# Three token columns per W2 chunk in group 0, a later first block of the tail, and three moved steps

## The chip, the cores and the metric

The kernel runs on one core of a Trainium2 chip. The metric is the device time of one execution in microseconds (us), smaller is better. One execution of the kernel before was also recorded by the hardware profiler; times "at 75.26" are us from the start of that record's span.

## What is computed

Inputs are q, k, v of shape (8, 8, 576, 64) in float32 (batch, heads, tokens, head size), a gain vector of 512, W1 (512 x 2048) and W2 (2048 x 512). The output is (8, 576, 512) in float32.

```python
# causal attention in a sliding window of 64 tokens
scores = scale * np.matmul(q, k.transpose(0, 1, 3, 2))
rel = pos[:, None] - pos[None, :]
mask = (rel >= 0) & (rel < 64)
attn = softmax(np.where(mask, scores, -1e9))
x = np.matmul(attn, v).transpose(0, 2, 1, 3).reshape(B, S, H * D)
# a layer norm and a two-layer MLP with a residual
mu = np.mean(x, axis=-1, keepdims=True)
var = np.mean((x - mu) ** 2, axis=-1, keepdims=True)
xn = (x - mu) / np.sqrt(var + 1e-06) * g_ln
out = x + np.maximum(xn @ w_ch1, 0.0) @ w_ch2
```

## The kernel before

**Groups and blocks.** The first 512 tokens of each of the 8 batches make groups 0 to 7; the last 64 tokens of all batches together make group 8, the tail. A group has four blocks of 128 tokens. Attention is done block by block, then the MLP for the group's 512 tokens at once. Matrix operands are float16, sums are float32.

**Attention of a block (g, j).** `s_mm` (L260) makes the scores on TensorE into two PSUM banks "sc" (for group 0 after a first product that writes the mask's bias), and ScalarE turns each bank into `pt` by Exp (L293). `s_mask` multiplies `pt` by the mask on VectorE. `b_step` (L302) multiplies `pt` by the values (16 products, L320) into the bank `xps`, of which there is one, and VectorE divides and takes mean and variance (L323 to L331). The values are there twice: `vA` has blocks of 128 tokens, `vB` the same rows shifted by 64 partitions. `z_step` normalizes the block, `zt_step` (L355) transposes it into `zT`, on TensorE with a copy out of PSUM for groups 0 and 1, by a transposing DMA on SP's queue from group 2 on. For groups 0 and 1 `vB` is filled by small copies on VectorE or ScalarE (`vB_cur`, `vB_prev`), which read the loaded float32 values `v32` directly; from group 2 on `make_vB` fills it from `vA` by two DMAs on GpSimd's queue. There is one buffer for `v32`, so `load_v` of a group waits until the group before has copied from it. GpSimd casts q, k, v, W1 and W2 from float32 to float16.

**MLP.** In groups 0 and 1 layer 1 runs in half tiles (`l1_half`, bank `hph`, tokens 0 to 255 and 256 to 511) and then whole ones (`l1`, bank `hps`); ScalarE applies Relu into `hrT`. Layer 2 of group 0 is four sums over 16 hidden chunks, one for each block of 128 tokens (a "token column", `ch`). W2 arrives in eight loads of two hidden chunks each, cast by `w2_cast` in that order. `l2_two` (L544) does columns 0 and 1 in step with the chunks, column 1 one chunk behind; `l2` does columns 2 and 3 after them. `add_out` adds the residual on VectorE and `store` issues the output DMA on SP. From group 1 on layer 2 is a Strassen-like form of seven products (`stage`, L492), in the order 1, 2, 6, 5, 7, 4, 3, two halves each; sums of operands are made on VectorE (`s_sums`, `w2_sums`), and several products add into one bank, with `post` (L482) on VectorE reading it in between. In the tail layer 1 has seven products too (`l1_product`, L560), on sums `zS` (`z_sums`, L695) and `w1S`.

**PSUM.** Eight banks: two "sc" (`ps_s`), two for `xps`, two for transposes ("t0" and "t1", `ps_t`), two "mm" (`ps_mm`) for products. `t_tile` (L74) alternates t0 and t1; while `tbank["shared"]` is set it uses t0 alone, since a product sits in t1.

**Order.** Every engine works through its instructions in the order in which the program writes them. The order is written by hand: the MLP of group g is a list of `units`, and `at(i, f, ...)` (L837) puts a step of the attention of the next group, a load or a cast behind unit i. Group 0 has 16 units of layer 1 (0 to 15), 9 of `l2_two` (16 to 24) and 8 of `l2` (25 to 32). Group 7 has 16 units of layer 1 and 14 of `stage`. `begin_last` (L822) starts the tail inside group 7; the rest of the tail runs from the generator `plan`. `keep_clock` puts extra products on TensorE during the start.

Of the kernel before, what the change touches and what calls it, by code (L numbers as in the profile page):

```python
# [10 lines left out]
FP32 = mybir.dt.float32  # L11
# [9 lines left out]
def kernel(  # L21
# [10 lines left out]
    nc = tc.nc  # L32
    B, H, S, D = q.shape
    DM = H * D
# [222 lines left out]
                    nc.tensor.transpose(out=tp[:, r, hp, :], in_=src[:, r, 2 * hp:2 * hp + 2, :], identity=ident16)  # L257
        evac(0, tailT[i][x], tp)

    def s_mm(g, j, pe_mask=False):  # L260
        sc = [ps_s.tile([128, NHP, 2, 64], FP32, tag="sc", name=f"sc_{g}_{j}_{par}") for par in range(2)]
        pt = p_pt.tile([128, 2, NHP, 2, 64], FP16, tag="pt", name=f"pt_{g}_{j}")
        pts[(g, j)] = pt
        if pe_mask:
            m = mbias[:, :]
            mb = bass.AP(tensor=m.tensor, offset=m.offset, ap=[m.ap[0], [0, NHP * 2], m.ap[1]])
            for par in range(2):
                nc.tensor.matmul(
                    out=sc[par][:, :].rearrange("p h w i -> p (h w) i"), lhsT=ident16, rhs=mb,
                    start=True, stop=False, skip_group_check=True,  # L270
                )
        for hp in range(NHP):
            for iw in range(2):
                for par in range(2):
                    rows = slice(64 * par, 64 * par + 64)
                    if g == NGRP - 1:
                        lhsT = tailT[j][1][rows, iw, hp, :]
                        rhs = tailT[j][0][rows, hp, 64 * iw:64 * iw + 64]
                    else:
                        w = 2 * j + iw  # L280
                        lhsT = qkT[g][1][rows, hp, 64 * w:64 * w + 128]
                        rhs = qkT[g][0][rows, hp, 64 * w:64 * w + 64]
                        if g >= XQ:
                            qb = flat(g)[rows, SM * hp + 16 * w:SM * hp + 16 * w + 16]
                            rhs = bass.AP(tensor=qb.tensor, offset=qb.offset, ap=[qb.ap[0], [128, 4], [1, 16]])
                    nc.tensor.matmul(out=sc[par][:, hp, iw, :], lhsT=lhsT, rhs=rhs,  # L286
                                     start=not pe_mask, stop=True, skip_group_check=pe_mask)
        for par in range(2):
            o, i = pt[:, par], sc[par][:, :]
            if XQ <= g < NGRP - 1:  # L290
                o = o.rearrange("p h w (r j) -> p (h w) r j", j=4)
                i = i.rearrange("p h w (j r) -> p (h w) r j", j=4)
            nc.scalar.activation(out=o, in_=i, func=AF.Exp, bias=0.0, scale=scale)  # L293

    def s_mask(g, j):
        pt = pts[(g, j)]
# [91 lines left out]
            eng.tensor_scalar(out=ab, in0=ab, scalar1=-1.0, scalar2=1.5, op0=ALU.mult, op1=ALU.add)  # L388
            eng.tensor_tensor(out=rs, in0=rs, in1=ab, op=ALU.mult)

    def mlp_units(g, split=0, two=False, seven=True):
        hrT = p_hrt.tile([128, NHC, 512], FP16, tag="hrT", name=f"hrT_{g}")
        hv = hrT[:, :, :].rearrange("p (c e) t -> p c e t", e=2)
        sS = {}
# [24 lines left out]
        def add_out(kb):  # L419
            xv = x_norm[(g, kb // 2)][:, kb % 2, :]  # L420
            if g < 2:
                nc.vector.scalar_tensor_tensor(
                    out=xv, in0=ch[kb], scalar=rstd[g][:, kb:kb + 1], in1=xv, op0=ALU.mult, op1=ALU.add,
                )
            else:
                nc.vector.tensor_tensor(out=xv, in0=ch[kb], in1=xv, op=ALU.add)
            store(kb)
# [113 lines left out]
            nc.scalar.activation(out=hrT[:, 2 * i:2 * i + 2, 256 * half:256 * half + 256], in_=hps,  # L541
                                 func=AF.Relu, bias=0.0, scale=1.0)

        def l2_two(i):  # L544
            for kb in range(2):
                e = i - kb
                if e == 0:
                    ch[kb] = ps_mm.tile([128, DM], FP32, tag="mm", name=f"ch_{g}_{kb}")
                if 0 <= e < NHC // 2:
                    for hc in (2 * e, 2 * e + 1):  # L550
                        nc.tensor.matmul(
                            out=ch[kb], lhsT=hrT[:, hc, 128 * kb:128 * (kb + 1)], rhs=w2s[:, hc, :],
                            start=(hc == 0), stop=(hc == NHC - 1),
                        )
                if e == NHC // 2 - 1:
                    add_out(kb)

        lbank = {}

# [31 lines left out]
        def l1_quad(d, e, h):  # L591
            return hv[:, 2 * d:2 * d + 2, e, 256 * h:256 * h + 256]
# [10 lines left out]
            eng.tensor_scalar(out=o, in0=o, scalar1=0.0, scalar2=None, op0=ALU.max)  # L603

        def l1_a(d):
            l1_product(1, d)
            l1_keep("s1", "A", d)
            l1_product(2, d)
            l1_sum(l1_quad(d, 0, 0), "B", "s1", d)
            l1_product(5, d)  # L610
            l1_keep("s5", "C", d)

# [13 lines left out]

        if last:
            def plan():
                yield
                l1_b(0)  # L630
                for d in range(1, 4):
                    l1_a(d)
                    l1_c(d - 1)
                    l1_b(d)
                    l1_e(d - 1)
                    if d == 2:
                        s_sums(0, 4, 1)
                stage(1, 0)
                s_sums(0, 4, 2)
                l1_c(3)  # L640
                s_sums(4, 8, 1)
                stage(1, 1)
                l1_e(3)
                s_sums(4, 8, 2)
                stage(2, 0)
                stage(2, 1)
                stage(6, 0)
                s_sums(0, 4, 3)
                stage(6, 1)
                s_sums(4, 8, 3)  # L650
                stage(5, 0)
                s_sums(0, 4, 4)
                stage(5, 1)
                s_sums(4, 8, 4)
                for n in (7, 4, 3):
                    for p in range(2):
                        stage(n, p)
                yield
            l1_a(0)
            return plan(), s_sums  # L660

        for half in range(2):
# [2 lines left out]

        for hc in range(split, NHC):
            units.append(lambda hc=hc: l1(hc))
        if two:
            for i in range(NHC // 2 + 1):
                units.append(lambda i=i: l2_two(i))  # L670
        if not seven:
            for kb in range(2 if two else 0, 4):
                for part in range(4):
                    units.append(lambda kb=kb, part=part: l2(kb, part))
        else:
            for n in (1, 2, 6, 5, 7, 4, 3):
                for p in range(2):
                    units.append(lambda n=n, p=p: stage(n, p))
# [86 lines left out]
    cast_qk(0, 1)  # L765
    cast_v(0, 2, 3)
    cast_v(0, 3, 4)
    for i in range(8):
        w1_cast(i)

# [21 lines left out]
    vB_prev(0, 2, 0)  # L792
    s_mm(0, 2, True)
    zt_step(0, 0)
    vB_cur(0, 3, 0)
    zt_step(0, 1)
    b_step(0, 2)
    s_mm(0, 3, True)
    z_step(0, 2)


# [20 lines left out]
    def begin_last():  # L822
        nonlocal rest
        rest, _ = mlp_units(NGRP - 1)
        next(rest)

    rest = None
    TAILS = {3: [0], 5: [1], 7: [2, 3]}
    for g in range(NGRP):
# [11 lines left out]
        if g == 0:  # L841
            at(0, b_step, 0, 3)
            at(1, zt_step, 0, 2)
            at(3, zt_step, 0, 3)
            at(4, newton, 0, 0, 4)
            at(11, t_main, 1, 0, 0, 1)
            at(12, t_main, 1, 1, 0, 1)
            at(13, vB_cur, 1, 0, 1)
            at(13, vB_prev, 1, 0, 1)
            at(13, vB_cur, 1, 1, 1)  # L850
            at(13, vB_prev, 1, 1, 1)
            at(16, s_mm, 1, 0)
            at(16, s_mask, 1, 0)
            at(17, s_mm, 1, 1)
            at(17, s_mask, 1, 1)
            at(18, b_step, 1, 0)
            at(21, b_step, 1, 1)
            at(22, zt_step, 1, 0)
            at(25, zt_step, 1, 1)
            at(26, t_main, 1, 0, 1, 0)  # L860
            at(27, t_main, 1, 1, 1, 1)
            at(28, vB_cur, 1, 2, 0)
            at(28, vB_prev, 1, 2, 1)
            at(29, vB_cur, 1, 3, 0)
            at(29, s_mm, 1, 2)
            at(29, s_mask, 1, 2)
            at(30, s_mm, 1, 3)
            at(30, s_mask, 1, 3)
            at(30, load_v, 2, 0, 4)
            at(33, b_step, 1, 2)  # L870
        if g == 1:
            at(0, cast_qk, 2, 0)
            at(0, cast_qk, 2, 1)
# [59 lines left out]
                at((2, 7, 12, 17)[j], z_step, b, j)  # L933
                at((12, 12, 18, {3: 24, 5: 23}.get(b, 22))[j], zt_step, b, j)
        for n, i in enumerate(TAILS.get(g, ())):
            ts = (13, 13, 16, 21) if n else (1, 2, 5, 11)
            at(ts[0], s_mm, NGRP - 1, i)
            at(ts[1], s_mask, NGRP - 1, i)
            at(ts[2], b_step, NGRP - 1, i)
            at(ts[2], z_step, NGRP - 1, i)  # L940
            at(ts[3], zt_step, NGRP - 1, i)
# [34 lines left out]
        if g == NGRP - 2:  # L976
            at(0, w1_sums, 1, 2)
            at(3, w1_sums, 3)
            at(21, w1_sums, 4)
            at(26, z_sums, NGRP - 1, 1, 2)  # L980
            at(27, z_sums, NGRP - 1, 3, 4)
            at(27, begin_last)
        for i, u in enumerate(units):
            if g > 1 and i == 20:
                tbank["shared"] = True
            u()
            for f, a in slots[i]:
                f(*a)
# [30 lines left out]
```

## Time and profile before

| | |
|---|---|
| median of 4 runs | 310.26 us (309.7 to 310.4) |
| the profiled execution: its time | 310.56 us |
| the profiled execution: span | 308.4 us |
| instructions in the span | 7582 |
| granted TensorE clock | 0.999 |
| VectorE, ScalarE, GpSimd busy | 218.1, 151.8, 170.9 us |
| moved by DMA | 58.35 MB, mean 189 GB/s |

The span runs from the first to the last recorded instruction; 2.16 us of the profiled execution lie around it. Rows of the profile have the form: line, engine, operation, output<-inputs by the program's names, shape, count; then busy time and the mean of one, and the idle time of the engine ahead of them with what ended it. PE is TensorE's products, PEld its weight loads, DVE is VectorE, ACT is ScalarE, POOL is GpSimd, SP is SyncE; SPq and POOLq are those engines' DMA issues. A wait is put down to what ended last. Line numbers are those of the kernel before.

### The profile page before, as it was taken

How to read it: one execution, taken by the hardware profiler on the slowest of the kernel's cores; microseconds unless marked ns; L12 is line 12 of the kernel's file. 1: busy time of each engine (PE TensorE's matmuls, PEld its weight loads, DVE VectorE, ACT ScalarE, POOL GpSimd, SP SyncE). 2: the span in 40 equal slices, each digit the busy share in tenths (PEclk: the TensorE clock that was granted, in tenths of full speed). 3: DMA queues.
4: the chain of work that ended last, by engine and by line, in shares of the span. 5: the costliest groups of instructions: out<-in, count | busy, mean ns of one | idle time of the engine just before them, and what ended most of it. 6: DMA issues, size and time to landing. Idle time of an engine off the chain costs nothing.

```text
span 308.4 us, 7582 instructions
## 1 busy us (share of the span) xinstructions
PE 296.2 (96%) x3061; PEld 196.8 (64%) x3061; DVE 218.1 (71%) x411; ACT 151.8 (49%) x255; POOL 170.9 (55%) x255
## 2 busy tenths in 40 slices
PE   7988989999999999999999999999999999999992
PEld 4557545697454478646954786469646854688882
DVE  0677575865775996589666965896669675868972
ACT  2496635587326742866157527752475056215500
POOL 7578676555861798279805983698145507104300
PEclk9999999999999999999999999999999999999999
DMA  8999899999866997899289997983790396003014
GB/s 191 266 384 306 309 361 271 276 273 252 166 170 201 237 204 137 274 289 120 51 263 285 216 143 237 297 153 72 219 168 20 60 204 180 19 17 138 0 37 102
DMA packets 113669, 58.35 MB, mean 189 GB/s; under 512 B 83617, under 2 KB 104609, under 8 KB 113634
## 3 DMA queue, kind: packets, MB, share of 16 engines
q1 hardware_dynamic: 112576, 54.67, 72.4%
q0 software_dynamic: 768, 2.80, 3.8%
q8 instruction: 24, 0.39, 0.6%
q10 hardware_dynamic: 290, 0.40, 0.4%
q14 instruction: 11, 0.09, 0.1%
HBM read 38.80 MB, written 9.44 MB: 156 GB/s over the span
## 4 chain that ended last, share of the span: by engine, by line
PE 75%; DMA 15%; SPq 5%; DVE 1%; POOL 1%; issue 1%; POOLq 0%
PE hps L400 28%; PE pA L477 12%; PE pB L477 8%; PE pC L477 8%; PE ch L412 6%; DMA w2s<-in_moe_w_ch_dram 5%; DMA qk<-in_q_dram 4%; SPq L141 4%; PE xps L320 3%; PE sc L286 3%; DMA vB<-vA 3%; PE lA L586 2%; PE tp L229 2%; DMA w1s<-in_moe_w_ch_dram 2%; DMA v<-in_v_dram 1%; SPq L89 1%
## 5 line engine op out<-in xcount | busy, mean ns | idle before, releaser
L400 PE MATMUL hps<-zT,w1g 128*128 128x512 f16 x416 | 95.3, 379 | 0.0
L404 ACT ACTIVATE hrT<-hps 128x512 f16<-128x512 f32 x104 | 62.3, 599 | 39.3 <-PE hps L400 35.7
L400 PEld LDWEIGHTS <-w1g 128*128 128x128 f16 x416 | 38.6, 98 | 43.3 <-issue 0.7
L293 ACT ACTIVATE pt<-sc 128x512 f16<-128x512 f32 x72 | 39.0, 594 | 27.8 <-DVE xn L484 14.7
L477 PEld LDWEIGHTS <-sS 128*128 128x128 f16 x448 | 43.3, 98 | 5.8 <-issue 0.9
L350 POOL TENSOR_SCALAR rsz<-mvg 128x1 f32<-128x1 f32 x28 | 10.2, 363 | 60.2 <-DVE mvg L331 59.5
L128 POOL CAST qk<-qk 128x1024 f16<-128x1024 f32 x32 | 35.0, 1107 | 12.6 <-DMA qk<-in_q_dram 4.3
L477 PEld LDWEIGHTS <-hrT 128*128 128x128 f16 x336 | 32.4, 98 | 5.5 <-ACT hrT L625 0.3
L300 DVE TENSOR_TENSOR pt<-pt,mask 128x1024 f16<-128x1024 f16 x32 | 26.9, 847 | 9.0 <-ACT pt L293 9.0
L215 ACT COPY qkT<-tp 128x1024 f16<-128x1024 f16 x16 | 16.1, 1012 | 34.1 <-PE tp L229 34.0
L484 DVE TENSOR_TENSOR xn<-pA,xn 128x512 f32<-128x512 f32 x28 | 19.2, 684 | 17.4 <-PE pA L477 12.1
L477 PE MATMUL pA<-wT,sS 128*128 128x256 f16 x224 | 26.9, 272 | 0.7 <-DVE xn L484 0.7
L477 PE MATMUL pC<-w2s,sS 128*128 128x256 f16 x224 | 26.9, 273 | 0.0
L353 POOL TENSOR_SCALAR z<-xn,rsz 128x512 f16<-128x512 f32 x28 | 25.0, 893 | 2.9
L323 DVE RECIPROCAL rcp<-xps 128x8 f32<-128x8 f32 x36 | 7.4, 204 | 26.3 <-PE xps L320 26.3
L328 DVE BATCH_NORM_STATS2 stats<-xn 128x6 f32<-128x512 f32 x36 | 25.0, 694 | 1.2
L326 DVE TENSOR_TENSOR xn<-xps,rcp 128x512 f32<-128x512 f32 x36 | 24.9, 691 | 1.2
L451 DVE TENSOR_TENSOR sS<-hrT 128x512 f16<-128x512 f16 (+1 forms) x40 | 24.5, 612 | 0.6 <-ACT hrT L404 0.6
L536 PE MATMUL hph<-zT,w1g 128*128 128x256 f16 x192 | 23.3, 273 | 0.8 <-ACT zT L368 0.8
L412 PE MATMUL ch<-w2s,hrT 128*128 128x512 f16 x96 | 23.1, 380 | 0.0
L147 POOL CAST vA<-v 128x1024 f16<-128x1024 f32 (+2 forms) x19 | 17.3, 929 | 6.8 <-DMA v<-in_v_dram 6.8
L320 PEld LDWEIGHTS <-pt 128*64 128x64 f16 x576 | 12.2, 110 | 13.3 <-issue 5.9
(111 smaller groups left out, 444.7 us busy)
## 6 DMA issues: line engine op xcount, KB each, us to landing
out_dram<-xn SPq DMA_DIRECT2D x33, 256.0 KB, 2.4
qk<-in_q_dram SPq DMA_DIRECT2D x16, 512.0 KB, 6.3
qk<-in_k_dram SPq DMA_DIRECT2D x16, 512.0 KB, 7.1
v<-in_v_dram SPq DMA_DIRECT2D x32, 256.0 KB, 7.2
w2s<-in_moe_w_ch_dram SPq DMA_DIRECT2D x9, 512.0 KB, 9.3
w1s<-in_moe_w_ch_dram SPq DMA_DIRECT2D x4, 512.0 KB, 6.7
tk<-in_k_dram SPq DMA_DIRECT2D x8, 256.0 KB, 4.7
tv<-in_v_dram SPq DMA_DIRECT2D x8, 256.0 KB, 5.0
```

The costliest lines, as they stand in the source:

```text
L128: nc.gpsimd.tensor_copy(out=dst[:, :].rearrange("p (a j) e d -> p a e j d", j=j), in_=t[:, :].rearrange("p (a e j d) -> p a e j d", e=2, j ...
L293: nc.scalar.activation(out=o, in_=i, func=AF.Exp, bias=0.0, scale=scale)
L300: nc.vector.tensor_tensor(out=ptv, in0=ptv, in1=mb, op=ALU.mult)
L326: nc.vector.tensor_tensor(out=xn, in0=xps[:, :, 0:D], in1=rcp_b, op=ALU.mult)
L328: nc.vector.bn_stats(out=stats, in_=xv)
L353: nc.gpsimd.tensor_scalar(out=z, in0=xv, scalar1=rs, scalar2=nm, op0=ALU.mult, op1=ALU.add)
L400: nc.tensor.matmul(out=hps, lhsT=w1g[:, kc, 128 * hc:128 * (hc + 1)], rhs=zT[g][:, kc, :], start=(kc == 0), stop=(kc == NKC - 1),)
L404: nc.scalar.activation(out=hrT[:, hc, :], in_=hps, func=AF.Relu, bias=0.0, scale=1.0)
L412: nc.tensor.matmul(out=ch[kb], lhsT=hrT[:, hc, 128 * kb:128 * (kb + 1)], rhs=w2s[:, hc, :], start=(hc == 0), stop=(hc == NHC - 1),)
L451: nc.vector.tensor_tensor(out=o, in0=x, in1=y, op=op)
L477: nc.tensor.matmul(out=o, lhsT=a[:, c, 128 * p:128 * p + 128], rhs=wv[:, c, :], start=(first and (p == 0 or split_c) and c == 0), stop=(c ...
L536: nc.tensor.matmul(out=hps[:, e], lhsT=w1g[:, kc, 128 * hc:128 * (hc + 1)], rhs=zT[g][:, kc, 256 * half:256 * half + 256], start=(kc == 0) ...
```

## The change

- Group 0, layer 2: `l2_three` takes columns 0, 1 and 2 in step with the W2 chunks, each one chunk behind the one before. Column 2 accumulates in t1, so the transposes of group 1 use t0 alone from unit 17 until column 2 has ended (unit 25). Column 3 follows in four units. The list has 30 units instead of 33, and the steps of group 1 behind it are put 1 to 3 slots earlier.
- Start: the scores of block 3 of group 0 go into the two "mm" banks (`later`), ahead of `b_step(0, 2)` and `zt_step(0, 1)`; their two Exps are issued after `zt_step(0, 1)`. The vB copy of block 3 (64 rows) leaves ScalarE; the diff writes it on GpSimd, ahead of the casts of W1. The copy of block 3's `zT` out of PSUM goes from ScalarE to VectorE.
- Group 7: `b_step`, `z_step` and `zt_step` of the tail's block 3 are one slot later.
- Tail: `z_sums` are one slot later; of `l1_a(0)` the products 1 and 2 stay at slot 27, product 5 goes to slot 28, behind the first half of product 3 of group 7.

```diff
+    def s_mm(g, j, pe_mask=False, later=False):
+        sc = [(ps_mm if later else ps_s).tile([128, NHP, 2, 64], FP32, tag="mm" if later else "sc",
+                                              name=f"sc_{g}_{j}_{par}") for par in range(2)]
...
+        if later:
+            return exps
+        exps()
...
-        def l2_two(i):
-            for kb in range(2):
+        def l2_three(i):
+            for kb in range(3):
                 e = i - kb
-                if e == 0:
+                if e == 0 and kb == 2:
+                    ch[kb] = ps_t.tile([128, DM], FP32, tag="t1", name=f"ch_{g}_{kb}")
+                elif e == 0:
                     ch[kb] = ps_mm.tile([128, DM], FP32, tag="mm", name=f"ch_{g}_{kb}")
...
                 if e == NHC // 2 - 1:
                     add_out(kb)
+                    if kb == 2:
+                        tbank["shared"] = False
...
         def l1_a(d):
+            l1_a1(d)
+            l1_a2(d)
+
+        def l1_a1(d):
             l1_product(1, d)
             l1_keep("s1", "A", d)
             l1_product(2, d)
             l1_sum(l1_quad(d, 0, 0), "B", "s1", d)
+
+        def l1_a2(d):
             l1_product(5, d)
             l1_keep("s5", "C", d)
...
             def plan():
+                l1_a2(0)
                 yield
...
-            l1_a(0)
+            l1_a1(0)
             return plan(), s_sums
...
     cast_v(0, 3, 4)
+    nc.gpsimd.tensor_copy(out=vB[0][64:128, 3, :, 0:D], in_=v32[0][0:64, 3])
...
     s_mm(0, 2, True)
     zt_step(0, 0)
-    vB_cur(0, 3, 0)
+    exps3 = s_mm(0, 3, True, True)
+    b_step(0, 2)
     zt_step(0, 1)
-    b_step(0, 2)
-    s_mm(0, 3, True)
+    exps3()
     z_step(0, 2)
...
-        next(rest)
...
-            at(3, zt_step, 0, 3)
+            at(3, zt_step, 0, 3, "dve")
...
-            at(21, b_step, 1, 1)
-            at(22, zt_step, 1, 0)
-            at(25, zt_step, 1, 1)
-            at(26, t_main, 1, 0, 1, 0)
-            at(27, t_main, 1, 1, 1, 1)
-            at(28, vB_cur, 1, 2, 0)
-            at(28, vB_prev, 1, 2, 1)
-            at(29, vB_cur, 1, 3, 0)
-            at(29, s_mm, 1, 2)
-            at(29, s_mask, 1, 2)
-            at(30, s_mm, 1, 3)
-            at(30, s_mask, 1, 3)
-            at(30, load_v, 2, 0, 4)
-            at(33, b_step, 1, 2)
+            at(20, b_step, 1, 1)
+            at(21, zt_step, 1, 0)
+            at(23, zt_step, 1, 1)
+            at(24, t_main, 1, 0, 1, 0)
+            at(25, t_main, 1, 1, 1, 1)
+            at(25, vB_cur, 1, 2, 0)
+            at(25, vB_prev, 1, 2, 1)
+            at(26, vB_cur, 1, 3, 0)
+            at(27, s_mm, 1, 2)
+            at(27, s_mask, 1, 2)
+            at(28, s_mm, 1, 3)
+            at(28, s_mask, 1, 3)
+            at(27, load_v, 2, 0, 4)
+            at(30, b_step, 1, 2)
...
-            ts = (13, 13, 16, 21) if n else (1, 2, 5, 11)
+            ts = (13, 13, 17, 22) if n else (1, 2, 5, 11)
...
-            at(26, z_sums, NGRP - 1, 1, 2)
-            at(27, z_sums, NGRP - 1, 3, 4)
+            at(27, z_sums, NGRP - 1, 1, 2)
+            at(28, z_sums, NGRP - 1, 3, 4)
             at(27, begin_last)
+            at(28, lambda: next(rest))
...
-            if g > 1 and i == 20:
+            if i == (20 if g > 1 else 17 if g == 0 else -1):
                 tbank["shared"] = True
```

More of the change, by code (lines that the diff above doesn't have):

```diff
@@ L258, in t_tail @@
         evac(0, tailT[i][x], tp)
-    def s_mm(g, j, pe_mask=False):
-        sc = [ps_s.tile([128, NHP, 2, 64], FP32, tag="sc", name=f"sc_{g}_{j}_{par}") for par in range(2)]
+    def s_mm(g, j, pe_mask=False, later=False):
+        sc = [(ps_mm if later else ps_s).tile([128, NHP, 2, 64], FP32, tag="mm" if later else "sc",
+                                              name=f"sc_{g}_{j}_{par}") for par in range(2)]
         pt = p_pt.tile([128, 2, NHP, 2, 64], FP16, tag="pt", name=f"pt_{g}_{j}")
@@ L287, in s_mm, with exps @@
                                      start=not pe_mask, stop=True, skip_group_check=pe_mask)
[L288 to L293, printed above, removed]
+        def exps():
+            for par in range(2):
+                o, i = pt[:, par], sc[par][:, :]
+                if XQ <= g < NGRP - 1:
+                    o = o.rearrange("p h w (r j) -> p (h w) r j", j=4)
+                    i = i.rearrange("p h w (j r) -> p (h w) r j", j=4)
+                nc.scalar.activation(out=o, in_=i, func=AF.Exp, bias=0.0, scale=scale)
+        if later:
+            return exps
+        exps()
     def s_mask(g, j):
@@ L389, in newton, with mlp_units @@
             eng.tensor_tensor(out=rs, in0=rs, in1=ab, op=ALU.mult)
-    def mlp_units(g, split=0, two=False, seven=True):
+    def mlp_units(g, split=0, three=False, seven=True):
         hrT = p_hrt.tile([128, NHC, 512], FP16, tag="hrT", name=f"hrT_{g}")
@@ L667, in mlp_units @@
             units.append(lambda hc=hc: l1(hc))
-        if two:
-            for i in range(NHC // 2 + 1):
-                units.append(lambda i=i: l2_two(i))
+        if three:
+            for i in range(NHC // 2 + 2):
+                units.append(lambda i=i: l2_three(i))
         if not seven:
-            for kb in range(2 if two else 0, 4):
+            for kb in range(3 if three else 0, 4):
                 for part in range(4):
```

## The prediction

> **What bounds the kernel now.** I read the page's engine line first, then TensorE's own waits, then the chain of waits around the longest DMA in it, then the timelines of the stages that the edits touch. All times are us from the span's start, of one profiled execution.
>
> ```profile
> PE 296.2 (96%) x3061; PEld 196.8 (64%) x3061; DVE 218.1 (71%) x411; ACT 151.8 (49%) x255; POOL 170.9 (55%) x255
> PE warm L749 <- DVE mbias L742: 2.3, 1, 2.3
> PE ztp L365 <- DVE z L342: 1.1, 1, 1.1
> PE hph L536 <- ACT zT L368: 0.8, 1, 0.8
> PE pA L477 <- DVE xn L484: 0.7, 1, 0.7
> PE ch L551 <- POOL w2s L204: 0.7, 2, 0.5
> PE xps L320 <- DMA vB<-vA: 0.4, 1, 0.4
> ```
>
> TensorE is busy for 96% and this list is nearly all that it waits for before its last product. The edits do not change how many products it runs, so they can win at most four of these lines: 1.1 (at 18.0), 0.8 (at 25.5), 0.7 (at 43 to 45) and, in group 7, 0.7 (at 268). Together 3.3. The line that decides is the last one: a wait of 0.41 that no edit names.
>
> ```profile
> 45.68 1.05 POOL w2s L204
> ...
> 54.02 1.25 DVE vB L217
> ...
> 55.85 0.92 SPq L141
> ...
> 56.82 3.82 SPq L141
> ...
> 60.69 4.03 DMA v<-in_v_dram
> ...
> 64.86 1.91 POOL vA L147
> ...
> 67.06 8.06 DMA vB<-vA
> 75.12 0.14 issue
> 75.26 0.45 PE xps L320 x16
> ```
>
> This is the chain of waits (start, length). Block 0 of group 2 (`b_step(2, 0)`, slot 14 of group 1) cannot start before vB of group 2 has landed at 75.12; TensorE's product before it ends at 74.85. So whatever is won before 75 is kept only as far as that landing moves. The chain says that v's load begins after VectorE's vB copy at 54 to 55.3. But it stays in its queue: the last of four issues is held until 60.69. The window table says why (columns: stretch, PE, PEld, DVE, ACT and POOL busy, clock, DMA share, GB/s):
>
> ```profile
> 52.00:54.00 2.00, 2.00 (x26) 0.87 (x23) 1.88 (x2) 0.98 (x2) 1.10 (x2) 1.00 1.03 337
> 54.00:56.00 2.00, 1.93 (x32) 0.90 (x25) 1.93 (x2) 1.36 (x3) 0.98 (x1) 1.00 0.93 280
> 56.00:58.00 2.00, 2.00 (x26) 0.97 (x24) 1.16 (x2) 0.81 (x2) 1.48 (x2) 1.00 1.08 405
> 58.00:60.00 2.00, 2.00 (x32) 1.64 (x30) 1.90 (x5) 0.79 (x2) 1.46 (x4) 1.00 1.19 301
> 60.00:62.00 2.00, 2.00 (x30) 1.79 (x23) 1.90 (x5) 1.24 (x3) 0.00 (x0) 1.00 0.43 99
> ```
>
> The DMA engines are full (share 0.93 to 1.19) up to 60. The loads of q and k for group 2 were issued by 50.8 and are landing until 57.4 (GpSimd's casts wait for them), then three stores, then v; v's packets of 256 bytes start only at 58.0 although v was issued at 55.4. An earlier issue waits in the same line.
>
> **The change part by part.**
>
> *Start.* `s_mm(0,3)` (2 + 16 products, 0.88) moves ahead of `b_step(0,2)` and `zt_step(0,1)`, into ps_mm. It fills the 1.08 wait before `ztp` at 19.02. But its two exps now stand behind the copy of zT block 1 on ScalarE, and the first `hph` takes over one of its banks. ScalarE: exps of block 2 to 18.77, zT 0 to 19.3, (the 0.62 vB copy gone), zT 1 to 20.1, first exp of block 3 to 20.6. So `hph` starts at 20.65, before at 20.60: nothing won there; the other exp ends at 21.15, hidden by the first `hph` (0.87).
>
> *vB copy of block 3.* The title says VectorE; the diff writes `nc.gpsimd.tensor_copy`. No row has GpSimd copying across partitions; priced as its cast 128x512, 0.62 (bounds 0.5 and 1.2), between 15.80 and w1's cast at 16.65 (idle 0.85 there). VectorE runs `z` (0.49) in the same place. In the trace such pairs stretch the VectorE side: z takes 0.87 at 24.22 with GpSimd busy, 0.49 at 15.77 without. The Trainium skill's "SBUF — State Buffer" (Who interferes with whom) speaks against the edit more strongly: an exclusive lock, the later one blocks fully. By the row w1's casts keep their time; by the rule the copy ends at 16.9 and the first four casts are 0.3 late. Either is covered by the 1.21 that GpSimd waits for w1's DMA at 20.72; without that cover it costs 0.3.
>
> *zT of block 3 on VectorE.* Before, the ScalarE copy stood behind a Relu (25.74, 0.58). `b_step(0,3)` is some 0.3 earlier, z ends near 24.75, transposes by 25.0. The copy from PSUM on VectorE: 128x1024 f16 takes 1.22, so 0.61 (bounds 0.4 to 0.9). Second half of layer 1 starts at about 25.75 instead of 26.37: 0.62 won. Newton stands behind it and is not needed before 47.
>
> *Three columns.* Layer 2 starts at 37.04 instead of 37.66. Six products per chunk, 0.217 each (four last 0.86 in the chain), give 1.30 per unit. With masks, blocks and transposes between, chunks 2 to 7 are wanted at 39.3, 41.0, 42.3, 44.0, 45.5 and 46.8; the casts end at 39.2, 40.5, 41.9, 43.6, 45.4 and 46.7. The 0.67 of waits is gone. New wait: column 2 sits in bank t1. `t_main(1,1,1)` at slot 25, after `shared` is cleared, takes t1 and waits for `add_out(2)` (0.74) on VectorE: TensorE stands from 50.1 to 50.9; k's cast, which ends at 50.39, would hold it there for 0.4 anyhow. Queued behind it: the last 16 products, two `s_mm`, `b_step(1,2)`; 5.04 in all. Group 1 starts at 56.4 instead of 57.84: 1.4 ahead. zt and q's transposes share t0 in turn; ScalarE empties it in 0.58 under 1.3 of products.
>
> *`load_v(2)`.* Its four DMAs keep their place on SP (after store 2, ahead of store 3). vB copies are done near 53.95 instead of 55.26, so it is issued 1.3 earlier. By the queue above v still lands near 64.7: bounds 0 and 1.3 earlier; I take 0 to 0.2, since the share had a little room (0.93) at 54 to 56. Then TensorE is at `b_step(2,0)` at 73.4 and waits 1.8. Longest wait inside the trace: 1.08, at clock 1.00. The Trainium skill's "TensorE: Matmul & The Clock Gate" (Part 1) halves the clock after an idle window of about 3.4: by that 1.8 costs nothing; if it did halve for such a window, an estimate by that page is 1.7 lost.
>
> *Group 7 and the tail.*
>
> ```profile
> 266.44 0.69 DVE L326 TENSOR_TENSOR xn<-xps,rcp 128x512 f32<-128x512 f32 x1
> 267.16 0.69 DVE L328 BATCH_NORM_STATS2 stats<-xn 128x6 f32<-128x512 f32 x1
> 267.89 0.18 DVE L331 BATCH_NORM_AGGREGATE mvg<-stats 128x2 f32<-128x6 f32 x1
> 267.99 0.67 DVE L484 TENSOR_TENSOR xn<-pA,xn 128x512 f32<-128x512 f32 x1
> 268.72 1.91 PE L477 MATMUL pA<-wT,sS 128*128 128x256 f16 x16 [0.73 <-DVE xn L484]
> ```
>
> Product 6 adds into bank A and waits for `post`, which waits behind the four VectorE instructions of `b_step(8,3)` (0.20 + 0.69 + 0.69 + 0.18). One slot later `post` comes first: 266.3 to 267.0, and product 6 follows at 267.99: 0.73 won. The block's statistics end near 268.85 (0.8 later), GpSimd's z (0.19, 0.55, 0.27, 0.98 and gaps) at 271.2, its transpose on SP lands (2.43) at 273.7; wanted by `z_sums` at 276.2. SP and GpSimd have nothing else in line there until 277.
>
> `z_sums(1,2)` move behind `post` B; product 5 behind the first half of product 3. VectorE: posts of product 7 to 275.5, B to 276.2, t1 at 276.6; product 5 comes at 276.7. So the split hides the sum: cost 0 if VectorE is on time, up to 0.4 if it is late; before, product 5 came 0.05 late. `z_sums(3,4)`: t3 at 278.1, wanted near 280. Everything to the end moves by 0.73 to 0.8, the last stores with it.
>
> Sum: before 75, 0 to 0.2 (0.1); after 250, 0.75; 0.85 in all. Span 308.4 to 307.55. The profiled execution took 310.56, 2.16 around its span, and is 0.30 above the median of 310.26; against the median this gives 309.4.
>
> **The rivals.**
> - *V moves along.* If the early issue does bring v forward, up to 1.3 before 75 is kept: 0.75 + 1.3, 308.2. For it: the chain of waits runs through that copy. Against: the full DMA share, and packets 2.6 after their issue.
> - *Slower.* Bank t1: if `add_out(2)` or t0's copies hold the transposes of k, then the kT copy (1.22) and vB copy (1.25) behind them on VectorE make `load_v(2)` late. v's packets start at 58.0[...], so from an issue at 56.0 on, each us late is one lost at 75. My sum has it at 54.0, so the transposes would have to slip by over 2.7 to eat the 0.75 too. With a slip of 4: 1.3 more in front of 0.75, 310.8. Against: VectorE idles for 3.09 at that place.
> - *Nothing left.* VectorE is late for t1 at 276.6 and the split wins nothing, product 5 and what follows losing the 0.73: 310.1. For it: t1 is on time by only 0.1. Against: a late t1 holds product 5 alone, and VectorE has no other work before it.
>
> **How the numbers follow.** My forecast 0.68 (309.0 to 309.8), v moving along 0.14 (308.0 to 309.0), nothing left 0.10, slower 0.08. About 0.2% (0.62) is what a measurement of this kernel can tell from no change; runs lie within 0.7 of each other, so of my forecast a quarter falls within it. Faster: 0.68 x 0.72 + 0.14 = 0.63, less 0.03 for ends that I could not bound; same: 0.19 + 0.10 = 0.29; slower 0.11. The range, 308.2 to 310.3, takes in most of the second and the third case.
>
> **What would show it.** Right: the wait of `xps` for `vB<-vA` grows from 0.4 to about 1.8 while group 1 starts at 56.4; `ch` waits for w2s no more; v's cast still starts near 64.8; `pA <- xn` is gone from TensorE's waits; product 5 starts within 0.1 of the half before it. Wrong: `xps` at that place starts before 74.5 (v moved along), or after 75.6 (slower); a new wait over 0.3 behind 275.

## The result, and the profile after

The changed kernel takes 309.39 us (median of 43 runs, 308.38 to 313.63), the kernel before 310.36 (62 runs, 309.27 to 312.76). The ratio is 0.9965, with an interval of 0.9957 to 0.9974: 0.97 us less by the medians, 1.1 (0.8 to 1.3) by the ratio. The forecast was 309.4. One of the 43 runs, the 313.63, was in a slower state, and the ratio leaves it out. The span of the profiled executions went from 308.36 to 307.54.

TensorE's row of the page, and then TensorE's own waits (total, times, longest), of the changed kernel:

```profile
PE 295.9 (96%) x3061; PEld 196.6 (64%) x3061; DVE 220.6 (72%) x412; ACT 150.6 (49%) x253; POOL 172.8 (56%) x256
```

```profile
PE warm L767 <- DVE mbias L760: 2.9, 1, 2.9
PE hph L543 <- ACT pt L296: 1.2, 1, 1.2
PE tp L229 <- DVE xn L429: 0.8, 1, 0.8
PE hph L543 <- DVE zT L377: 0.5, 1, 0.5
PE hph L543 <- DVE xn L429: 0.2, 1, 0.2
```

Of the old list, `pA <- xn`, `ch <- w2s` and `xps <- vB` are gone. Three lines are new: the first `hph` waits for an exp of block 3 (1.2, where `ztp` waited 1.1), `tp` of group 1's keys waits for the bank t1 (0.8), and an `hph` of group 1 waits for column 3's bank (0.2). The `hph` that waited for ScalarE's copy of `zT` (0.8) waits for VectorE's (0.5). The line that was to grow, `xps <- vB`, does not exist. The wait of `warm`, ahead of everything, is 0.6 longer, and no edit touches it.

Where the 0.82 of the span lies is read from five landmarks, the starts of TensorE's instructions in the timelines (us):

| kernel | first `hph` | first `ch` | group 1's first `hph` | block 0 of group 2 | first `lA` (tail) | last product ends | span |
|---|---|---|---|---|---|---|---|
| before | 20.60 | 37.66 | 57.84 | 75.26 | 275.70 | 302.72 | 308.36 |
| after | 21.64 | 38.05 | 58.00 | 75.42 | 274.95 | 301.91 | 307.54 |

The changed kernel is 1.04 behind at the first `hph` and still 0.16 behind at block 0 of group 2. From there to the first `lA` it takes 199.53 instead of 200.44, and from `lA` to the end of the last product 26.96 instead of 27.02. So 0.91 and 0.06 are won in group 7 and the tail, and 0.16 is lost in front. This is the place in group 7 (start, length): one line of TensorE's timeline before, then TensorE's and VectorE's timelines after.

```profile
266.08 1.91 PE L477 MATMUL pB<-w2s,hrT 128*128 128x256 f16 x16
```

```profile
266.21 1.92 PE L484 MATMUL pB<-w2s,hrT 128*128 128x256 f16 x16
267.96 1.91 PE L484 MATMUL pA<-wT,sS 128*128 128x256 f16 x16
...
275.39 0.60 PE L597 MATMUL lB<-zT,w1g 128*128 128x256 f16 x4
275.82 1.04 PE L484 MATMUL pC<-w2s,sS 128*128 128x256 f16 x8
276.70 0.60 PE L597 MATMUL lC<-zsums,w1S 128*128 128x256 f16 x4
```

```profile
266.35 0.68 DVE L491 TENSOR_TENSOR xn<-pA,xn 128x512 f32<-128x512 f32 x1
266.95 0.20 DVE L330 RECIPROCAL rcp<-xps 128x8 f32<-128x8 f32 x1
...
276.20 0.41 DVE L726 TENSOR_TENSOR zsums<-zT 128x512 f16<-128x512 f16 x1
```

The `post` of bank A now stands ahead of the block's reciprocal, and product 6 (`pA`) follows 1.75 after the start of product 4 (`pB`) with no wait beside it; before, product 6 started at 268.72, 2.64 after it. In the tail the half of product 3 (`pC`, 8 products) runs while `zsums` is formed until 276.61; `lC`, the fifth product, comes at 276.70.

### The profile page after: what moved, and what is told of

The parts are those of the page before. It is cut to its first block, busy times and chain, and to the rows that moved or that the text cites. A ratio compares the mean times of both kernels' runs of the same rounds, so it can differ in the third digit from the quotient of the medians.

```text
span 307.5 us, 7582 instructions
## 1 busy us (share of the span) xinstructions
PE 295.9 (96%) x3061; PEld 196.6 (64%) x3061; DVE 220.6 (72%) x412; ACT 150.6 (49%) x253; POOL 172.8 (56%) x256
## 4 chain that ended last, share of the span: by engine, by line
PE 94%; ACT 2%; DVE 1%; POOL 0%; issue 0%; POOLq 0%; ACTq 0%
PE hps L407 30%; PE pA L484 12%; PE pB L484 8%; PE pC L484 8%; PE hph L543 7%; PE ch L419 5%; PE xps L327 4%; PE sc L287 4%; PE tp L229 4%; PE ch L560 3%; PE lA L597 2%; PE warm L767 2%; ACT pt L296 2%; PE lC L597 1%; PE ztp L372 1%; PE sc L269 1%
## 5 line engine op out<-in xcount | busy, mean ns | idle before, releaser
L407 PEld LDWEIGHTS <-w1g 128*128 128x128 f16 x416 | 38.6, 98 | 43.3 <-issue 0.7
L128 POOL CAST qk<-qk 128x1024 f16<-128x1024 f32 x32 | 35.9, 1135 | 10.2 <-DMA qk<-in_k_dram 4.5
L543 PEld LDWEIGHTS <-w1g 128*128 128x128 f16 x192 | 18.0, 98 | 4.7 <-POOL w1g L190 1.3
L358 POOL TENSOR_TENSOR rsz<-rsz,mhalf 128x1 f32<-128x1 f32 x28 | 19.4, 691 | 2.3
```

Of the source, the lines that this page charges most:

```text
L128: nc.gpsimd.tensor_copy(out=dst[:, :].rearrange("p (a j) e d -> p a e j d", j=j), in_=t[:, :].rearrange("p (a e j d) -> p a e j d", e=2, j ...
L407: nc.tensor.matmul(out=hps, lhsT=w1g[:, kc, 128 * hc:128 * (hc + 1)], rhs=zT[g][:, kc, :], start=(kc == 0), stop=(kc == NKC - 1),)
L543: nc.tensor.matmul(out=hps[:, e], lhsT=w1g[:, kc, 128 * hc:128 * (hc + 1)], rhs=zT[g][:, kc, 256 * half:256 * half + 256], start=(kc == 0) ...
```

## The experiments

Three theories are named in the expectations.
- **Theory A** is the prediction: the landing of vB of group 2 pins all that lies before 75, so the gain is made after 250.
- **Theory B** came from the first look at the profile above: vB landed at 74.06, 1.06 earlier than before, so group 0's edits may carry a good part of the gain, and the late start (first product at 2.91 instead of 2.31) hid it in this one execution.
- **Theory C** was formed after the first four runs: nothing waits for vB; the lead of group 0 is spent sooner, at bank t1, at the bank that column 3 still holds, and at z of block 2 of group 1.

**The change in two halves.** The first run is the kernel before with only group 7's and the tail's edits, these lines with `l1_a` split into `l1_a1` and `l1_a2`. The second is the changed kernel with the same lines back to the old ones, so that only the start and the three columns are left.

```diff
-            ts = (13, 13, 16, 21) if n else (1, 2, 5, 11)
+            ts = (13, 13, 17, 22) if n else (1, 2, 5, 11)
...
-            at(26, z_sums, NGRP - 1, 1, 2)
-            at(27, z_sums, NGRP - 1, 3, 4)
+            at(27, z_sums, NGRP - 1, 1, 2)
+            at(28, z_sums, NGRP - 1, 3, 4)
             at(27, begin_last)
+            at(28, lambda: next(rest))
```

> The kernel before with the edits of group 7 and the tail alone (tail block 3 one slot later, z_sums one slot later, product 5 split off). Theory A (the landing of vB for group 2 pins everything before 75, so the gain is made after 250): 0.9 less than before, all of the change's gain but 0.1. Theory B (group 0's edits carry a good part of it, since vB landed at 74.06 instead of 75.12 in the profile after): 0.9 less here too, but then group 0 alone must add to it. If the two parts add up, this ratio is 0.997.

> The change without its edits of group 7 and the tail: start and three columns alone. Theory A: 0 to 0.2 less than before, and a wait of xps for vB<-vA of about 1.8 where TensorE starts as early as in the profile before. Theory B: 0.4 to 0.9 less, with no wait for vB<-vA and its landing before 74.5. A loss of up to 0.3 would mean that the wait for bank t1 (0.84 in the profile after) costs more than the waits for W2 that it replaces.

Measured: the tail's edits alone 309.48, ratio 0.9969 (0.9953 to 0.9985); group 0's edits alone 310.42, 1.0008 (0.9994 to 1.0022). The tail carries the whole, and Theory B falls as to the time. The waits of TensorE with group 0's edits alone keep the old stall of group 7, under the new one of bank t1:

```profile
PE tp L229 <- DVE xn L429: 0.8, 1, 0.8
PE pA L484 <- DVE xn L491: 0.7, 1, 0.7
```

With the tail's edits alone group 0 is the old one, but vB landed at 74.53 (75.12 before) and nothing waits for it. That is the first sign that the 0.41 of the profile of before is no fixed part of that kernel.

**The late start taken away.** In the profile after, `mbias` takes 0.97 on VectorE instead of 0.37, and all of the start is 0.6 to 1.0 late. These two kernels form it on GpSimd, one from the kernel before, one from the changed one:

```diff
-    nc.vector.tensor_scalar(out=mbias, in0=mask, scalar1=-1.0, scalar2=30000.0, op0=ALU.add, op1=ALU.mult)
+    nc.gpsimd.tensor_scalar(out=mbias, in0=mask, scalar1=-1.0, scalar2=30000.0, op0=ALU.add, op1=ALU.mult)
```

> The kernel before with the mask's bias mbias written by GpSimd instead of VectorE. In the profiles mbias took 0.37 (before) and 0.97 (after) on VectorE, both from 1.88, with GpSimd's memsets beside it, and TensorE's first product came at 2.31 or 2.91; 0.9 of it was left at 16. If this is chance in each execution of both kernels, the first product comes at 2.3 to 2.5 always. Theory A: no change to 0.3 less, since the wait of 0.41 for vB covers part of a late start. Theory B the same.

> The changed kernel with mbias written by GpSimd. Theory A: TensorE reaches block 0 of group 2 at 73.4 to 74.5 and waits there for vB; 0 to 0.3 less than the changed kernel (309.1 to 309.4). Theory B: nothing waits there, so the 0.9 of the early start is kept to the end wherever an execution started late: 308.5 to 308.9.

Measured: 310.22, 0.9992 (0.9978 to 1.0005), and 309.42, 0.9974 (0.9956 to 0.9993). The first product starts at 2.24 and 2.23. The pair is worth no measurable time, but it gives two profiles with the same start, in which the lead of group 0 can be followed:

| kernel | first `hph` | first `ch` | group 1's first `hph` | block 0 of group 2 |
|---|---|---|---|---|
| before, `mbias` on GpSimd | 20.23 | 37.53 | 58.15 | 75.16 |
| after, `mbias` on GpSimd | 20.55 | 37.31 | 57.27 | 75.02 |

A lead of 0.22 at layer 2 and of 0.88 at group 1 is down to 0.14 at block 0. One pair is good to a few tenths only: the six executions of kernels with the old group 0 start group 1 between 57.69 and 58.31. TensorE's timeline of the second kernel shows what takes it (idle time before the instruction and its releaser in brackets):

```profile
51.76 0.61 PE L229 MATMUL tp<-ident,qk 128*128 128x128 f16 x8 [0.84 <-DVE xn L429]
...
58.54 1.03 PE L543 MATMUL hph<-zT,w1g 128*128 128x256 f16 x8 [0.23 <-DVE xn L429]
...
61.19 0.40 PE L372 MATMUL ztp<-ident,z 128*128 128x128 f16 x4 [0.26 <-DVE z L349]
...
75.02 0.22 PE L327 MATMUL xps<-vB,pt 128*64 128x65 f16 x1
```

The 0.84 is the bank t1; it was paid before group 1, so the 0.88 is what is left after it. The rest goes behind it: an `hph` needs the bank that column 3 holds until its `add_out` (0.23 in the bracket), and z of block 2 of group 1 is not ready for its transpose (0.26). The brackets understate both. From group 1's first `hph` to block 0 it is 16.93 where neither is waited for (the tail's edits alone), 17.42 in the changed kernel, which waits for the first only, and 17.75 here: 0.49 and 0.33. In the kernel before with `mbias` on GpSimd the stretch is 17.01. The 0.08 more than 16.93 are put down to vB, which landed there at 75.03: block 0 starts 0.13 behind that, and 0.14 behind it in the profile of before, where it waits. Together this is the 0.74 by which the lead shrinks. At 75 no wait for vB is left in the second kernel, where vB had landed at 74.38. This gave Theory C.

The wait for column 3's bank is no mark of the new columns alone: it stands in all executions with them, and in two of the seven with the old columns (0.23 and 0.19, below in the block's slots and in the split).

**A filler ahead of 75.** Eight `hph` products of group 1 are done twice in one chain; the second pass starts their sum anew, so the values stay. The size expected was 0.87; the `hph` products between the two `sc` around it take 4.47 instead of 3.72 in both kernels, so the filler is 0.75. If vB pins 75, a filler in the changed kernel is covered by the wait; if nothing waits for vB, it is not.

```diff
-                for kc in range(NKC):
+                for kc in 2 * list(range(NKC)) if (g, half) == (1, 1) and i == 3 else range(NKC):
```

> The kernel before with 8 products of hph (128x256) in unit 11 of group 1 done twice: 0.87 more TensorE work ahead of block 0 of group 2, same values. Theory A (the landing of vB holds what is won before 75): the wait of 0.4 covers part, so 0.4 to 0.5 more. Theory C (the landing of vB is not what limits; the lead is lost earlier): in before the wait of 0.41 is still there, so the same 0.4 to 0.9 more.

> The changed kernel with the same 8 products done twice. Theory A (TensorE comes 1.8 early to block 0 of group 2 and waits for vB): the filler is covered, 0 to 0.1 more than the changed kernel, ratio to before 0.9965 to 0.997. Theory C (the lead is spent at bank t1, at the bank that column 3 still holds, and at z of block 2 of group 1, so nothing waits for vB): the whole 0.87 is added, ratio 0.999 to 1.0.

Measured: 312.28, 1.0041 (1.0017 to 1.0065), and 311.21, 1.0021 (0.9998 to 1.0043). In the changed kernel block 0 of group 2 starts at 75.78, against 75.02 in an execution with as early a start (first product at 2.31 and 2.23) and no filler: all of the filler comes through. The cover of Theory A is not there. In the kernel before, block 0 moves from 75.26 to 75.51, by 0.25 only: the wait for vB is given up, which is 0.49 by the starts (17.42 from group 1 to block 0 instead of 16.93; 0.41 in the bracket).

At the end the fillers cost more than that, and more than either theory said: 1.3 and 1.7 by the ratios (the second against 0.9965). So the place of block 0 decides between the theories, not the time at the end. In the profiles the spans are 2.2 longer than those of before and of the changed kernel with `mbias` on GpSimd. Each profile has one new wait further on. This is the one of the changed kernel with the filler, at block 3 of group 5, which both kernels transpose on TensorE: TensorE's timeline, then GpSimd's.

```profile
183.30 0.40 PE L372 MATMUL ztp<-ident,z 128*128 128x128 f16 x4 [1.25 <-POOL z L360]
```

```profile
182.48 0.76 POOL L360 TENSOR_SCALAR z<-xn,rsz 128x512 f16<-128x512 f32 x1 [1.78 <-DMA zT<-z]
```

In the other it is 1.7, of the same kind. GpSimd's z waits for the transposing DMA of an earlier z. With the filler that DMA is issued on SyncE at 176.77 in the changed kernel and at 176.96 in the kernel before, and lands 5.6 later; without it, it is issued at 175.38 and 175.32 and lands 4.0 and 4.2 later. Why 0.8 and 0.3 at block 0 become 1.4 and 1.6 at that issue stays open.

**Can the lead be kept?** The first kernel (from the changed one, `mbias` on GpSimd) spreads the waiting steps further, some of them from the end of group 0 into group 1 (the lower half of the diff):

```diff
-            at(25, t_main, 1, 1, 1, 1)
-            at(25, vB_prev, 1, 2, 1)
+            at(26, t_main, 1, 1, 1, 1)
+            at(26, vB_prev, 1, 2, 1)
...
-            at(27, s_mm, 1, 2)
-            at(27, s_mask, 1, 2)
-            at(28, s_mm, 1, 3)
-            at(28, s_mask, 1, 3)
+            at(28, s_mm, 1, 2)
+            at(28, s_mask, 1, 2)
...
-            at(30, b_step, 1, 2)
...
-            at(1, b_step, 1, 3)
-            at(2, zt_step, 1, 2)
+            at(0, s_mm, 1, 3)
+            at(0, s_mask, 1, 3)
+            at(1, b_step, 1, 2)
+            at(3, b_step, 1, 3)
+            at(5, zt_step, 1, 2)
...
-            at(5, zt_step, 1, 3)
+            at(6, zt_step, 1, 3)
```

The second also sends block 0's rows of vB of group 2 as a DMA of their own, ahead of the other three:

```diff
-        nc.gpsimd.dma_start(out=vB[b][64:128, :], in_=vA[b][0:64, :])
+        for c in ((slice(0, 1), slice(1, 4)) if b == 2 else (slice(0, 4),)):
+            nc.gpsimd.dma_start(out=vB[b][64:128, c], in_=vA[b][0:64, c])
```

> The changed kernel with mbias on GpSimd and three waits behind column 2 taken away by order: the transposes of k (group 1, second half) one unit later, so that column 4's products run while add_out(2) reads t1; s_mm of blocks 2 and 3 one unit later; b_step of blocks 2 and 3 of group 1 at slots 1 and 3 of group 1, zt at 5 and 6, so that neither hph's bank nor z is waited for. Theory C: the lead of 1.4 that was forecast is there at the transposes (group 1 starts before 56.6), TensorE reaches block 0 of group 2 near 73.5 and now waits for vB until it lands at 74.4 to 75: 0 to 0.6 less than the changed kernel with mbias on GpSimd (309.42). Theory A: the same wait, and no gain at all.

> As the spread kernel, and make_vB of group 2 issues the rows of block 0 as a DMA of their own ahead of the rest (a quarter of the first transfer). If the landing of vB is what then holds TensorE, the smaller transfer lands up to 1 sooner and 0.3 to 1.0 more is won than by the spread alone. If nothing waits there, no change, or up to 0.1 more for the third DMA issue (0.53) on GpSimd's queue.

Measured: 309.63, 0.9972 (0.9952 to 0.9992), and 310.10, 0.9996 (0.9975 to 1.0017). In the first the waits only change their names (`ztp` for the copy of q and k 0.6, `hph` for column 3's bank 0.4, two of 0.2), and block 0 of group 2 stands at 75.26. In the second block 0 does start at 74.30, 0.96 ahead of the kernel before. Then TensorE's timeline has this:

```profile
94.35 2.79 PE L408 MATMUL hps<-zT,w1g 128*128 128x512 f16 x12 [0.83 <-DMA zT<-z]
```

The transposed z of group 2, which comes by a DMA, is late by 0.83 (0.90 by the starts), and 0.33 (0.40) are lost at 78.23, where a block waits for its masked `pt`. At the first `lA` the kernel stands at 275.14, 0.59 behind the changed one with `mbias` on GpSimd (274.55). So the lead won before 75 was lost again within twenty us. Whether the early arrival makes these waits, and by what, was not shown.

**One edit at a time**, each against the kernel before: the block's slots alone (`ts = (13, 13, 17, 22)`), the split of product 5 with the later `z_sums` alone, the start alone, the three columns with their slots alone.

The block's slots:

```diff
-            ts = (13, 13, 16, 21) if n else (1, 2, 5, 11)
+            ts = (13, 13, 17, 22) if n else (1, 2, 5, 11)
```

The split:

```diff
-            l1_a(0)
+            l1_a1(0)
...
-            at(26, z_sums, NGRP - 1, 1, 2)
-            at(27, z_sums, NGRP - 1, 3, 4)
+            at(27, z_sums, NGRP - 1, 1, 2)
+            at(28, z_sums, NGRP - 1, 3, 4)
...
+            at(28, lambda: next(rest))
```

The start:

```diff
+    nc.gpsimd.tensor_copy(out=vB[0][64:128, 3, :, 0:D], in_=v32[0][0:64, 3])
...
-    vB_cur(0, 3, 0)
-    zt_step(0, 1)
+    exps3 = s_mm(0, 3, True, True)
...
-    s_mm(0, 3, True)
+    zt_step(0, 1)
+    exps3()
...
-            at(3, zt_step, 0, 3)
+            at(3, zt_step, 0, 3, "dve")
```

The three columns, with the slots of group 0 as in the change:

```diff
-        def l2_two(i):
-            for kb in range(2):
+        def l2_three(i):
+            for kb in range(3):
...
-            if g > 1 and i == 20:
+            if i == (20 if g > 1 else 17 if g == 0 else -1):
```

> The kernel before with only the tail's block 3 one slot later in group 7. The wait of product 6 for bank A (0.73 in the profile before) should be gone. The prediction's size: 0.73 less. From the profile after, where product 6 starts 0.76 earlier although the product before it starts 0.13 later: 0.89 less, ratio 0.9971.

> The kernel before with only z_sums one slot later and product 5 of the tail's first unit split off. The prediction: 0 to 0.07 less, no change to be seen. If product 5 is late for its sum, up to 0.4 more; the place shows it as the time from the first lA to the second (3.12 before, 3.06 in the profile after).

> The kernel before with only the edits of the start (scores of block 3 ahead, vB copy on GpSimd, zT copy on VectorE). Half 2 of layer 1 was forecast 0.62 earlier; in the profiles with mbias on GpSimd it is 26.01 against 26.24, in the two without the tail's edits 26.53 and 26.37. Expected: 0.2 to 0.6 earlier there for an execution that starts equally early, and at the end no change (within 0.2), since the casts of W2 (46.7) are then waited for longer.

> The kernel before with only the three columns and their slots. The waits for W2 (0.7) go, the wait for bank t1 (0.8 to 1.0), that of hph for add_out (0.2) and that of zt for z (0.3) come: no change at the end, or up to 0.3 more. Were the forecast of the prediction right, group 1 would start 0.8 earlier than before and xps would wait 1.2 for vB.

| only this edit | median | ratio (interval) | block 0 of group 2 to `lA` | `lA` to the last product's end |
|---|---|---|---|---|
| block's slots | 309.51 | 0.9972 (0.9953 to 0.9991) | 199.83 | 27.03 |
| split of product 5 | 310.03 | 0.9998 (0.9979 to 1.0017) | 200.48 | 26.96 |
| start | 310.49 | 1.0018 (0.9994 to 1.0042) | 200.48 | 27.03 |
| three columns | 310.78 | 1.0021 (1.0001 to 1.0041) | 200.48 | 27.02 |

The slot of one block is the change. The split shows its 0.06 in the profile, and that is below what the runs can tell. The two edits of group 0 win nothing, each for itself; the three columns may even cost a little. In the first row, from product 4's start to product 6's it wins 0.88 (266.82 to 268.58, before 266.08 to 268.72), but its stretch from block 0 to product 4 is 0.27 longer than before. That is the wait for GpSimd's z that the fillers have, at 182.12: 0.09 by the bracket, 0.25 by the starts. Behind that place the size of the edit shows without it: from the transposes at 181 to 184 to the first `lA` it is 94.32 to 94.34 in the seven executions with the old slots and 93.43 or 93.44 in the seven with the new ones, 0.89 less.

The start alone shows why it needs the three columns beside it. TensorE's waits:

```profile
PE ch L558 <- POOL w2s L204: 1.4, 2, 1.1
```

Layer 2 begins 0.25 sooner (37.41), still takes its chunks of W2 two columns at a time, and so waits 1.4 for the casts instead of 0.7. W2's casts do not come sooner with it: the last two end at 45.84 and 47.33 in this execution and at 45.42 and 46.72 before, each behind its load. What the start wins is waited for there.

No version tried is better than the changed kernel beyond the intervals: its slots alone, its tail's edits alone, and the two with `mbias` on GpSimd and no extra DMA lie between 309.42 and 309.63.

## Why the prediction was right, and where it was not

The predicted time, 309.4, and the sign held, and so did the place: the gain is made after 250. Its parts hold less well than the total, and that the time agrees to 0.01 is luck: the forecast was counted from 310.26, the median of 4 runs, which is 310.36 in 62, and the gain is 0.97 where 0.85 was forecast. The two differences cancel.

**Group 7, mis-sized.** Forecast 0.73 for product 6; by the starts of products 4 and 6 it is 2.64 before and 1.75 after, so 0.89. The 0.73 was the idle time in the bracket of product 6's row, and this counts from an end of the product before it that is modelled. Such a chain of 16 lasts 1.75 from its start to the next product's where nothing waits (273.95 to 275.70, before); 268.72 less 266.08 less 1.75 would have given the 0.89. The later z did no harm, as forecast: VectorE's statistics end at 268.81 (forecast 268.85), GpSimd's z at 270.95 (271.2), wanted at 276.2.

**The split, right.** Cost 0 if VectorE is in time; `zsums` is done 0.09 before the product that reads it (forecast 0.1), and the 0.05 of lateness before is won (0.06).

**Group 0, right for a wrong reason.** The step that failed is "whatever is won before 75 is kept only as far as that landing moves". It took the 0.41 wait of one execution for a gate. vB's issue stands between 66.27 and 67.64 in the fourteen executions and its landing moves between 73.92 and 75.12, also where group 0 is the old one. Only the execution that the prediction was made from, where it lands last, shows TensorE waiting; in the next latest, 75.03, TensorE is held by the 0.08 named above, and in the other twelve not at all. So the predicted sign (`xps <- vB` growing to 1.8) did not appear, and the filler was not covered. What a lead of 1.4 would have met is not known, since no execution had one.

What stands in its place is that the forecast lead was too large, and that what there was of it was spent behind group 1's start. Forecast start of group 1: 56.4; with the early start of the execution it is 57.27, so 0.87 later. Two terms make the difference.
- The second half of layer 1 was to win 0.62 by the copy of zT on VectorE. The copy is faster than priced (0.42, forecast 0.61), and z is ready in time (24.59, forecast 24.75), but TensorE comes to the transposes only at 25.10, when they were to be over at 25.0. The half starts at 26.01, 0.23 sooner than in the kernel before with the same start, and 0.36 sooner than in the profile that the forecast was made from. Layer 2 starts 0.27 late by this (37.31, forecast 37.04).
- From there to the wait for bank t1 it takes 13.61, forecast 13.06. Four `ch` take 0.86 in a row and 0.97 where `sc` or `xps` follow. That 0.1 for each such switch was not in the sum, and there are four in this stretch; the rest of the 0.55 is not accounted for.

Then the third: a bank that `add_out` empties last was counted at t1 (0.8 forecast, 0.84 measured), but not at column 3, which an early `hph` of group 1 needs (0.49 by the starts), nor was z of block 2 (0.33). These two take most of the lead of 0.88. The rule that the prediction applied to one bank applies to the other as well.

**The DMA queue, right.** v of group 2 was forecast to be issued 1.3 earlier and to land as before. SyncE's queue and GpSimd's timeline, first of the changed kernel with `mbias` on GpSimd, then of the kernel before:

```profile
54.23 7.37 SPq L141 DMA_DIRECT2D v<-in_v_dram  x4
64.86 1.89 POOL L147 CAST vA<-v 128x2048 f16<-128x2048 f32 x1 [4.01 <-DMA v<-in_v_dram]
```

```profile
55.41 6.09 SPq L141 DMA_DIRECT2D v<-in_v_dram  x4
64.86 1.89 POOL L147 CAST vA<-v 128x2048 f16<-128x2048 f32 x1 [5.41 <-DMA v<-in_v_dram]
```

Issued 1.18 sooner, the load holds the queue 1.28 longer, and the cast that waits for it starts at the same time. In all fourteen executions the picture is the same: four issue v between 54.2 and 54.6 and cast it between 64.86 and 65.27, ten issue it between 54.9 and 56.0 and cast it between 64.07 and 65.44. The rival "V moves along" had its bound from this and fell by it.

**The rest.** The first `hph` won nothing, as forecast: 1.2 of `pt` in place of 1.1 of z (with `mbias` on GpSimd it even comes later, at 20.55 instead of 20.23). The vB copy on GpSimd took 0.61 at 15.84 (forecast 0.62 at 15.80) in the changed kernel and 0.68 at 15.89 with `mbias` on GpSimd, so it ended at 16.45 and 16.57, before the 16.9 that the prediction took from the lock. w1's casts began at 16.66 and at 17.06 (before 16.65). Both times GpSimd waited for w1's DMA behind them, 1.08 and 0.98, so the cover that the prediction named held. The waits for W2 went to nothing. The slip of bank t1 never came near the 2.7 of the slower rival. The wait of 1.8, for which the price of a slower clock was weighed, did not arise in the changed kernel. The nearest to it is the 1.74 at 183 in the kernel before with the filler: the granted clock stays at 1.00 there, and the chain of 16 behind it takes 1.74 (183.77 to 185.51). That wait cost nothing beyond itself.

## What to carry to other kernels

A wait of a few tenths in one profile is a sample: before it is made the gate of a forecast, its two sides, when the thing lands and when it is asked for, are to be looked at in a second execution or bounded by the spread of the transfer. What a stall on a chain of products is worth is read from the starts of its two ends less the chain's own length, not from the idle time that a row lists after a modelled end. In this kernel a lead won early was spent at the next thing that did not move with it, and the gain that stayed was the late one, with little behind it but the end.

## What the runs showed of the hardware

The start of VectorE's `mbias` and its neighbour on GpSimd, the memset of vB: VectorE's timeline before, VectorE's after, GpSimd's after.

```profile
1.88 0.37 DVE L742 TENSOR_SCALAR mbias<-mask 128x64 f16<-128x64 f16 x1 [0.83 <-POOL mask L738]
```

```profile
1.88 0.97 DVE L760 TENSOR_SCALAR mbias<-mask 128x64 f16<-128x64 f16 x1 [0.83 <-POOL mask L756]
```

```profile
2.22 0.60 POOL L151 MEMSET vB<- 64x520 f16 x1
```

The same instruction starts at the same 1.88 beside the same work of GpSimd, and ends at 2.25 in one execution and at 2.85 in the other, just after the memset of 2.22 to 2.82 ends. Of the executions with `mbias` on VectorE, two (the changed kernel and group 0's edits alone) have 0.97, the others 0.37, the changed kernel with the filler among them, whose start is the same code; formed on GpSimd it takes 0.24 at 1.94, and TensorE starts at 2.23 or 2.24. The memset takes 0.60 in the two and where `mbias` is not on VectorE, and 0.64 or 0.65 in the others, so it seems to stand still for the little that is left of `mbias` there. The Trainium skill's "SBUF — State Buffer" (Who interferes with whom) says that VectorE's `tensor_scalar` can take the port pair that it shares with GpSimd, and that the side which does not hold the pair stands still for the whole of the other's instruction. The 0.6 agrees with that in its length. By the same page whoever issues first gets the pair, and VectorE's row starts 0.34 ahead of the memset, so which side wins is not read from the starts. That the memset is the cause was argued from these times and not tried by itself. The late start is worth nothing at the end of this kernel, as the runs with `mbias` on GpSimd show.
